# An attention and gated-MLP block on one core: last additions on GpSimd, one weight scale a run later, the first rows in another order

## The chip, the cores and the metric

The kernel runs on one core of a Trainium2 chip, alone. The metric is the device time in microseconds (us); a time shown is the median of several runs. Besides these there is one profiled execution with a trace of every engine: TensorE (PE, with its weight loads PEld), VectorE (DVE), ScalarE (ACT), GpSimd (POOL) and SyncE (SP, which here only starts transfers). "Span" is the time from the first to the last instruction of that execution.

## The reference

Every output row is the input row plus an attention result, gated by an MLP:

```python
x  = A_x                                   # 1 x 2048 x 640
xn = layernorm(x)
q  = xn @ wq                               # 32 heads of 192
k, v = last 512 rows of the caches         # per head
o  = softmax(q @ k.T * 192 ** -0.5) @ v
s  = concat(o) @ wo                        # 6144 -> 640
h  = sigmoid(xn @ w_gate) * (xn @ w_up)    # 640 -> 1536
g  = silu(h @ w_down)                      # 1536 -> 640
return x + s * g
```

## The kernel before, in words

The order of the instructions on each engine is the order in which the program writes them; nothing is rearranged by a scheduler. Each engine works through its own list and waits on semaphores where an operand is not there yet. The program has four stages.

**Head and MLP (lines 273 to 541).** The 2048 rows are 16 tiles of 128. `load_x` (299) starts a transfer for each of the first four tiles on SP, between those of the first slices of the gate and up weights (`load_w`, 320); 324 to 332 set the order: x0, x1, gate 0, up 0, x2, gate 1, up 1, x3, gate 2, and so on. `ln_part` and `ln_stats` (346, 351) compute the statistics of a tile in two halves on DVE, `ln_sqrt` (392) the root on ACT, then follow the reciprocal and `ln_apply` (360) on DVE. `turn` (397) transposes the five 128-column blocks of the normalised tile on PE and copies them from PSUM to SBUF on ACT: for tile 0 in two copies, else in one. `first_mm(q, f)` (383) makes ten 128x128 products of row tile q with feature block f, five for gate and five for up. The loop at 407 weaves these for the first four tiles; `warm_up` (375) puts products of zeros on PE ahead of the first row and behind its transposes (`NWARM`, line 59). From feature block 3 on, all products are 512 columns wide (line 484), with a sigmoid on ACT (489) and a product on DVE (490) behind each.

**Attention (563 to 954).** 16 runs r = 0 to 15: eight groups of two head pairs, each for two halves of the rows (pi 0 and 1). A run has 16 slots k of score products (`stage_s`, 652, exponential on ACT, 667), woven with the query products of the next run (`products`, 569, whose results DVE copies or adds, lines 590 and 607), and then eight blocks of value products (`stage_pv`, 669), each with a division on DVE (683, 684), and a transpose and a store issued on SP (690, `store_o`, 693). `phase_s` (828) hangs other work on slots: in even runs `load_k` (157) on SP at slot 2 and `scale_k` (167) on DVE at slot 12 (14 in one of them), in odd runs the transposes of K (173), loads for later stages and so on.

Weights and keys are scaled by powers of two; for the query weights there is one scale for two groups. `scan_abs` (201) sums absolute values on ACT; `set_scan` (204) and `set_scale` (207) reduce them on DVE, write a 128x128 tile `mx_b` and have SP transpose it into `mx_row` (213); `set_scale2` (215) reduces that row on DVE and writes the scale and its inverse. The tables `sets` and `sets2` (750, 751) say in which (run, slot) the two parts stand. Scale 2 is for groups 4 and 5; its first user is `weights(4, 0)` (755) behind the second value block of run 5, on ACT and then on GpSimd.

**Output products (956 to 1167).** The output and down projections, 24 steps, each of seven block products (`product`, 1003, line 1007) on PE; `result` (1033) finishes one half (LEFT or RIGHT, 320 columns) of a row tile. In steps whose tile is finished it adds a part kept in SBUF (1060), multiplies by scale and gate (`gated`, 990, line 991) and adds `acc` (1062), all on DVE. Usually GpSimd starts the store of a whole tile (1066); in the last step SP starts one for each half (1064). The last half of the last step is made and finished in two quarters of 160 columns (1156 to 1159).

Of the kernel before, what the change touches and what calls it, by code (L numbers as in the profile page):

```python
# [9 lines left out]
ALU = mybir.AluOpType  # L10
# [7 lines left out]
def kernel(  # L18
# [13 lines left out]
    nc = tc.nc  # L32
    P = 128
    ctx.enter_context(tc.manual_schedule())

    xf = A_x.flatten_outer_dims()
    of = out.flatten_outer_dims()
    S, D = xf.shape
# [12 lines left out]
    NCD = D // P  # L51
# [4 lines left out]
    G = 2  # L56
    NG = NPAIR // G
    assert NG == 8 and HQDH == 48 * P and NST == 4
    NWARM = (9, 2)
    FA = 3  # L60
    PC = 3
    GC = 2 * G * DH
# [29 lines left out]
    DN = D // 2  # L92
    LEFT, RIGHT = slice(0, DN), slice(DN, D)
# [179 lines left out]
    with ExitStack() as bctx:  # L273
# [24 lines left out]

        def load_x(t):
            x_sb = xin_pool.tile([P, D], BF16, name=f"x_sb{t}")  # L300
            nc.sync.dma_start(x_sb[:], xf[t * P:(t + 1) * P, :])
            x_tiles[t] = x_sb[:]

        def load_x4(s):
# [15 lines left out]
        def load_w(w_sb, w_r, k):  # L320
            f = slice(f_cuts[k], f_cuts[k + 1])
            nc.sync.dma_start(w_sb[:, :, f], w_r[:, :, f])

        load_x(0)
        load_x(1)
        for k in range(len(f_cuts) - 1):
            load_w(wg_sb, wg_r, k)
            load_w(wu_sb, wu_r, k)
            if k < 2:
                load_x(2 + k)  # L330
            elif k == 3:
                load_x4(1)
# [13 lines left out]
        def ln_part(t, i):  # L346
            if i == 0:
                stats_t[t] = bwork.tile([P, nsub, nc.vector.BN_STATS_DIM], F32, name="stats")
            nc.vector.bn_stats(stats_t[t][:, i, :], x_tiles[t][:, i * fsz:(i + 1) * fsz])  # L349

        def ln_stats(t, i0=0):
            for i in range(i0, nsub):
                ln_part(t, i)
            nc.vector.bn_aggr(mv[:, t, :], stats_t[t][:])
# [5 lines left out]
        def ln_apply(t):  # L360
            xn = xpool.tile([P, D], BF16, name="xn")
            cuts = [0, 2 * P, D] if t == 0 else [0, D]
            for d in map(slice, cuts, cuts[1:]):
                nc.vector.tensor_scalar(  # L364
                    xn[:, d], x_tiles[t][:, d], mv[:, t, 0:1], rstd[:, t, :],
                    op0=ALU.subtract, op1=ALU.mult,
                )
            return xn
# [6 lines left out]
        def warm_up(n):  # L375
            for _ in range(n):
                nc.tensor.matmul(w_ps, lhsT=warm[:, 0:P], rhs=warm[:], start=True, stop=True)

        warm_up(NWARM[0])

        gu_first = [bank2() for _ in range(FA)]

        def first_mm(q, f):
            r = slice(q * P, (q + 1) * P)
            for i, w in enumerate((wg_sb, wu_sb)):
                for c in range(NCD):
                    nc.tensor.matmul(  # L387
                        gu_first[f][:, i, r], lhsT=w[:, c, f * P:(f + 1) * P], rhs=xnT[0][:, c, r],
                        start=(c == 0), stop=(c == NCD - 1),
                    )  # L390

        def ln_sqrt(q):
            nc.scalar.activation(
                rstd[:, q:q + 1, :], mv[:, q:q + 1, 1:2], AF.Sqrt, bias=eps_t[:], scale=1.0
            )

        def turn(q):
            pT = pT_banks[:, q % 2, 0:NCD * P // 2].bitcast(BF16).rearrange("p (c n) -> p c n", c=NCD)
            for c in range(NCD):
                nc.tensor.transpose(pT[:, c, :], xn_t[q][:, c * P:(c + 1) * P], ident[:])  # L400
            for cs in ((slice(0, 2), slice(2, NCD)) if q == 0 else (slice(0, NCD),)):
                nc.scalar.activation(xnT[0][:, cs, q * P:(q + 1) * P], pT[:, cs, :], AF.Copy)

        xn_t = {}
# [2 lines left out]
        for q in range(TQ):  # L407
            if q + 1 < TQ:
                ln_part(q + 1, 0)
            nc.vector.reciprocal(rstd[:, q:q + 1, :], rstd[:, q:q + 1, :])  # L410
            xn_t[q] = ln_apply(q)
            if q + 1 < TQ:
                ln_stats(q + 1, 1)
                ln_sqrt(q + 1)
            if q == 0:
                turn(0)
                warm_up(NWARM[1])
                continue
            first_mm(q - 1, 0)
            turn(q)  # L420
            first_mm(q - 1, 1)
            if q == 2:
                first_mm(0, 2)
                first_mm(1, 2)
            elif q == 3:
                first_mm(2, 2)
        for f in range(FA):
            first_mm(TQ - 1, f)
# [43 lines left out]
        for s in range(NST):  # L472
# [4 lines left out]
            for f in range(NF):  # L477
# [16 lines left out]
                if s + 1 < NST:  # L494
                    t = (s + 1) * TQ
# [251 lines left out]
    scans_pv.update({(4 + n, 7): 15 + n for n in range(NCD)})  # L747
    scans_load = {(0, 6): (11, 5), (1, 4): (12, 4), (2, 4): (13, 5), (3, 4): (14, 4)}
    scans_load.update({(4 + n, 4): (15 + n, 5 - n % 2) for n in range(NCD)})
    sets = {(1, 1): 1, (4, 1): 2, (9, 1): 3}  # L750
    sets2 = {(1, 12): 1, (5, 0): 2, (9, 12): 3}
    scale_s = {0: 2, 3: 3, 15: 4}
    q_after = {1: (0,), 2: (1,), 3: (2,), 4: (3,), 5: (4,), 6: (5, 6), 8: (7,), 10: (8,), 12: (9,), 14: (10,)}

# [24 lines left out]
    def tiles_of(j):  # L779
        kind, m = steps[j]  # L780
        if kind == "D":
            return (m, TQ + m) if m < TQ else (TQ + m, 2 * TQ + m)
        pi, q = divmod(m % 8, TQ)
        return [(2 * pi + i) * TQ + q for i in range(2)]
# [175 lines left out]
    acc = {t: acc_pool.tile([P, D], F32, name=f"acc{t}") for t in order}  # L960
# [29 lines left out]
    def gated(dst, src, gate):  # L990
        nc.vector.scalar_tensor_tensor(dst, src, descale, gate, op0=ALU.mult, op1=ALU.mult)  # L991
# [21 lines left out]
    def keep(b, dst):  # L1013
        nc.scalar.activation(dst, ps_all[:, b, 0:DN], AF.Copy)
# [9 lines left out]
    NP = len(steps)  # L1024
    tmp_at = [0, 0, 0]

    def turn_of(k, rows_):
        tmp_at[k] += 1
        return rows_[(tmp_at[k] - 1) % len(rows_)]
# [3 lines left out]
    def result(j, i, d, b, more, n0=0, n1=DN):  # L1033
        kind, m = steps[j]
        t = tiles_of(j)[i]
        ps, tt = ps_all[:, b, n0:n1], nc.vector.tensor_tensor
        if kind == "D":
            if t not in gate_of:
                gate_of[t] = turn_of(1, gate_rows)
            if more is not None:  # L1040
                v = turn_of(2, down_tmps)
                tt(v, ps, more[:], ALU.add)
                ps = v
            nc.scalar.activation(gate_of[t][:, d], ps, AF.Silu, scale=g_scale)
            if (i, d) in ((0, RIGHT), (1, LEFT)):
                nc.gpsimd.dma_start(gB_d[t * P:(t + 1) * P, :], gate_of[t])
            return
        d = slice(d.start + n0, d.start + n1)
        if m < 8:
            if more is None:  # L1050
                keep(b, acc[t][:, d])
            else:
                tt(acc[t][:, d], ps, more[:], ALU.add)
            return
        gate, o_sb = gx_rows[1, t]
        tmp = turn_of(0, tmps)[:, 0:n1 - n0]
        if more is None:
            gated(tmp, ps, gate[:, d])
        else:
            tt(tmp, ps, more[:], ALU.add)  # L1060
            gated(tmp, tmp, gate[:, d])
        tt(o_sb[:, d], tmp, acc[t][:, d], ALU.add)  # L1062
        if j == NP - 1:
            nc.sync.dma_start(of[t * P:(t + 1) * P, d], o_sb[:, d])
        elif (i, d) in ((0, RIGHT), (1, LEFT)):
            nc.gpsimd.dma_start(of[t * P:(t + 1) * P, :], o_sb)

# [30 lines left out]
    for j in range(NP):  # L1098
# [38 lines left out]
        side(j, 3)  # L1137
        product(j, Z, "A12", 3, True)
        result(j, 0, LEFT, Z, p1s)
        scales(4)  # L1140
        side(j, 4)
        product(j, X, "S3", 4, False)
        result(j, 1, RIGHT, X, p5s)
        scales(5)
        if more:
# [6 lines left out]
        side(j, 6)  # L1152
        product(j, Y, "S4", 5, False)
        result(j, 0, RIGHT, Y, u2s)
        side(j, 7)
        cuts = (0, DN) if more else (0, DN // 2, DN)
# [42 lines left out]
```

## Time and profile before

| what | value |
|---|---|
| runs of the kernel before | 871.42 us median of 3 (871.37 to 873.0) |
| profiled execution, its own time | 872.36 us |
| its span | 870.2 us |
| granted TensorE clock, mean | 0.999 |
| busy: PE, PEld, DVE, ACT, POOL | 863.0, 570.7, 674.5, 628.5, 234.3 us |
| first 512-column product of the MLP (L484) | 14.93 us |
| last product on PE begins / last DVE instruction ends | 866.0 / 867.48 us |
| last store issued (SP, L1064) | 867.51 us |

The times in the table's last three rows, and all times in timelines below, count from the start of the span. A line of a timeline reads: start in us, duration in us, engine, line of the program, operation, tile written <- tiles read, shapes, count of merged instructions, and in brackets how long the engine sat idle before and what released it. "SPq" is the time that SP's sequencer spends on starting a transfer. In the chain that ended last, each instant of the span is put down to the one instruction or transfer that the end was waiting for.

### The profile page before, as it was taken

To read this page: it belongs to the slowest core of one execution; us is meant where nothing else is said; L and a number is where in the kernel's file an instruction comes from. 1 tells how busy PE (TensorE), PEld (TensorE's weight loads), DVE (VectorE), ACT (ScalarE), POOL (GpSimd) and SP (SyncE) were. 2 spreads that over 40 slices of the span, in tenths; PEclk is the share of its full clock that TensorE was granted. 3 is DMA by queue.
4 is the path that set the end of the run, shared out by engine and by line. 5 is a ranking of instruction groups with operands and counts; after the bars stand their busy time and mean duration, and the time that the engine had idled before them with its cause. 6 is when DMAs were issued, how large, how long until landed. Compare 5 with 4: busy or idle time off the path is not lost.

```text
span 870.2 us, 19053 instructions
## 1 busy us (share of the span) xinstructions
PE 863.0 (99%) x7557; PEld 570.7 (66%) x7557; DVE 674.5 (78%) x1148; ACT 628.5 (72%) x783; POOL 234.3 (27%) x320
## 2 busy tenths in 40 slices
PE   9999999999999999999999999999999999999998
PEld 5444447576678676676676676676777777777775
DVE  6586767777877867867877867888788778889997
ACT  4766568899799799799789688647556566766552
POOL 0085076062362352352352452300000011000000
PEclk9999999999999999999999999999999999999999
DMA  9894993998998987998988967997795977676641
GB/s 280 188 248 113 240 244 82 236 138 236 219 158 233 256 170 194 223 172 225 206 144 214 199 106 193 237 206 248 163 277 179 300 240 224 212 269 222 226 134 35
DMA packets 258872, 175.97 MB, mean 202 GB/s; under 512 B 162976, under 2 KB 241440, under 8 KB 258784
## 3 DMA queue, kind: packets, MB, share of 16 engines
q1 hardware_dynamic: 253248, 157.26, 73.2%
q0 software_dynamic: 5536, 17.50, 10.0%
q8 instruction: 59, 0.97, 0.5%
q14 instruction: 29, 0.24, 0.1%
HBM read 101.71 MB, written 36.70 MB: 159 GB/s over the span
## 4 chain that ended last, share of the span: by engine, by line
PE 97%; DVE 1%; DMA 1%; SPq 0%; issue 0%; ACT 0%; DVEq 0%
PE ps_all L1007 26%; PE ps_all L569 21%; PE ps_all L677 20%; PE ps_all L663 19%; PE ps_all L484 11%; PE ps_all L387 1%; DMA kraw<-in_A_k_cache_dram 0%; DVE stats L349 0%; DVE arm L991 0%; DMA x_sb<-in_A_x_dram 0%; DVE arm L1062 0%; DVE arm L1060 0%; DVE qp L590 0%; DVE xn L364 0%; SPq L213 0%
## 5 line engine op out<-in xcount | busy, mean ns | idle before, releaser
L667 ACT ACTIVATE E<-ps_all 128x1024 bf16<-128x1024 f32 x256 | 251.4, 1023 | 92.4 <-PE ps_all L663 90.4
L663 PE MATMUL ps_all<-qT,kT 64*128 64x512 bf16 x1536 | 198.1, 376 | 0.0
L677 PEld LDWEIGHTS <-E 128*128 128x128 bf16 x2048 | 169.7, 98 | 9.2 <-issue 9.2
L677 PE MATMUL ps_all<-v_sb,E 128*128 128x193 bf16 x2048 | 174.3, 247 | 0.9 <-DVE qT L607 0.8
L607 DVE TENSOR_TENSOR qT<-ps_all,qp 128x512 bf16<-128x512 f32 x174 | 115.7, 688 | 48.2 <-PE ps_all L569 38.8
L1007 PEld LDWEIGHTS <-mid 128*128 128x128 f16 x1236 | 120.3, 98 | 46.0
L663 PEld LDWEIGHTS <-kT 64*128 64x128 bf16 x1536 | 86.5, 94 | 77.5 <-issue 3.5
L590 DVE COPY qp<-ps_all 128x512 f32<-128x512 f32 x150 | 100.5, 687 | 42.2 <-PE ps_all L569 42.2
L684 DVE TENSOR_TENSOR o_st<-ps_all,rden 128x768 bf16<-128x768 f32 x128 | 122.6, 958 | 4.4
L569 PE MATMUL ps_all<-mid 64*128 64x512 f16 (+1 forms) x840 | 106.3, 376 | 0.0
L569 PE MATMUL ps_all<-mid,arm 64*128 64x512 f16 (+1 forms) x840 | 105.5, 376 | 0.0
L569 PEld LDWEIGHTS <-mid 64*128 64x128 f16 x840 | 50.4, 94 | 42.0 <-issue 1.4
L569 PEld LDWEIGHTS <-arm 64*128 64x128 f16 x840 | 47.1, 94 | 44.6 <-issue 0.2
L1007 PE MATMUL ps_all<-arm,mid 128*128 128x320 f16 x480 | 70.4, 299 | 0.0
L808 ACT ACTIVATE mid<-mid,w_sc 128x1536 f16<-128x1536 bf16 (+1 forms) x43 | 61.4, 1451 | 0.0
L240 ACT ACTIVATE mid<-mid,w_sc 128x1536 f16<-128x1536 bf16 x37 | 58.1, 1571 | 1.1 <-DVE w_sc L218 0.7
L1007 PE MATMUL ps_all<-op,mid 128*128 128x320 f16 (+1 forms) x408 | 58.1, 295 | 0.0
L490 DVE TENSOR_TENSOR hT_sb<-ps_all,sig_sb 128x512 bf16<-128x512 f32 x48 | 32.8, 686 | 28.4 <-PE ps_all L484 20.8
L489 ACT ACTIVATE sig_sb<-ps_all 128x512 bf16<-128x512 f32 x48 | 28.4, 596 | 35.3 <-PE ps_all L484 33.8
L258 POOL TENSOR_TENSOR mid<-mid 128x384 f16<-128x384 f16 x20 | 18.1, 906 | 120.1 <-ACT mid L240 119.1
L1007 PE MATMUL ps_all<-mid 128*128 128x320 f16 x348 | 49.9, 299 | 0.0
L258 POOL TENSOR_TENSOR arm<-mid 128x384 f16<-128x384 f16 x20 | 18.1, 907 | 114.5 <-ACT mid L240 113.5
(183 smaller groups left out, 1093.1 us busy)
## 6 DMA issues: line engine op xcount, KB each, us to landing
oT_d<-oT SPq DMA_DIRECT2D x64, 384.0 KB, 4.9
mid<-oT_d SPq DMA_DIRECT2D x46, 384.0 KB, 4.0
mid<-in_A_wq_dram POOLq DMA_DIRECT2D x64, 192.0 KB, 6.7
arm<-in_A_wo_dram SPq DMA_DIRECT2D x16, 480.0 KB, 6.2
h_d<-hT_sb SPq DMA_DIRECT2D x16, 384.0 KB, 4.4
kraw<-in_A_k_cache_dram SPq DMA_DIRECT2D x32, 192.0 KB, 3.2
v_sb<-in_A_v_cache_dram SPq DMA_DIRECT2D x32, 192.0 KB, 5.5
arm<-in_A_wq_dram SPq DMA_DIRECT2D x15, 384.0 KB, 5.3
```

What stands on the lines that cost most here:

```text
L240: nc.scalar.activation(raw.bitcast(F16), raw, AF.Copy, scale=w_ups[g // 2])
L258: tt(TB, part_w(g, c, a, 1, 1), part_w(g, c, a, 0, 1), ALU.subtract)
L484: nc.tensor.matmul(gu[:, i, :], lhsT=w[:, c, f * P:(f + 1) * P], rhs=xnT[s][:, c, :], start=(c == 0), stop=(c == NCD - 1),)
L569: nc.tensor.matmul(ps_all[:, b, :], lhsT=w(r, c), rhs=x[r, c, :], start=(first and k == 0), stop=(k == len(cs) - 1), skip_group_check=True,)
L590: nc.vector.tensor_copy(dst, part(b))
L607: nc.vector.tensor_tensor(q_out(i, u, pp), part(b), t, ALU.add)
L663: nc.tensor.matmul(ps[:, b, :], lhsT=kT[h, c * PC + j, :], rhs=qT_t[r][i, j][h, pp, :], start=(j == 0), stop=(j == PC - 1),)
L667: nc.scalar.activation(E_t[r, i, pp][:, c, :, :], ps, AF.Exp, scale=scale_qk)
L677: nc.tensor.matmul(o_ps[:, q // 2, q % 2, 0:DH + 1], lhsT=E[:, c, h, q * P:(q + 1) * P], rhs=vt[:, c, 0:DH + 1], start=(c == 0), stop=(c = ...
L684: nc.vector.tensor_tensor(o_st[:, :, h * DH:(h + 1) * DH].rearrange("p (b i) d -> p b i d", b=2), o_ps[:, :, :, 0:DH], rden[:].to_broadcas ...
L808: eng.activation(t, t.bitcast(BF16), AF.Copy, scale=up)
L1007: nc.tensor.matmul(ps_all[:, b, d0:d1], lhsT=a[:, c, :], rhs=w[:, c, d0:d1], start=(start and c == 0), stop=(c == nk - 1), skip_group_chec ...
```

## The change

Four edits, quoted whole:

```diff
-    NWARM = (9, 2)
+    NWARM = (9, 1)
@@ load_x
-            nc.sync.dma_start(x_sb[:], xf[t * P:(t + 1) * P, :])
+            for d in (LEFT, RIGHT) if t == 0 else (slice(0, D),):
+                nc.sync.dma_start(x_sb[:, d], xf[t * P:(t + 1) * P, d])
@@ turn
-            for cs in ((slice(0, 2), slice(2, NCD)) if q == 0 else (slice(0, NCD),)):
+            for cs in (slice(0, 2), slice(2, NCD)):
@@ loop over the first four tiles
             xn_t[q] = ln_apply(q)
+            for f in {1: (0,), 2: (0, 1), 3: (0,)}.get(q, ()):
+                first_mm(q - 1, f)
             if q + 1 < TQ:
                 ln_stats(q + 1, 1)
+            if q == 2:
+                ln_sqrt(3)
+            turn(q)
+            if q < 2:
                 ln_sqrt(q + 1)
             if q == 0:
-                turn(0)
                 warm_up(NWARM[1])
-                continue
-            first_mm(q - 1, 0)
-            turn(q)
-            first_mm(q - 1, 1)
-            if q == 2:
+            elif q == 1:
+                first_mm(0, 1)
+            elif q == 2:
                 first_mm(0, 2)
                 first_mm(1, 2)
-            elif q == 3:
+            else:
+                first_mm(2, 1)
                 first_mm(2, 2)
@@ the tables of the scales
-    sets = {(1, 1): 1, (4, 1): 2, (9, 1): 3}
-    sets2 = {(1, 12): 1, (5, 0): 2, (9, 12): 3}
+    sets = {(1, 1): 1, (5, 1): 2, (9, 1): 3}
+    sets2 = {(1, 12): 1, (5, 12): 2, (9, 12): 3}
@@ result
-        tt(o_sb[:, d], tmp, acc[t][:, d], ALU.add)
+        if j == NP - 1 and more is not None:
+            nc.gpsimd.tensor_tensor(o_sb[:, d], tmp, acc[t][:, d], ALU.add)
+        else:
+            tt(o_sb[:, d], tmp, acc[t][:, d], ALU.add)
         if j == NP - 1:
-            nc.sync.dma_start(of[t * P:(t + 1) * P, d], o_sb[:, d])
+            eng = nc.scalar if i == 0 and d.start > 0 or n0 == 0 and n1 < DN else nc.sync
+            eng.dma_start(of[t * P:(t + 1) * P, d], o_sb[:, d])
```

In words. **Head:** the first tile of x comes in two transfers of 320 columns, so SP starts one transfer more; every tile's transposed rows are copied in two parts; on ACT the copies of tiles 0 and 1 now stand ahead of the root of the next tile, while the root of tile 3 still stands ahead of the copies of tile 2; on PE the product of tile 1 with feature block 1 now stands ahead of the transposes of tile 2, and one product of zeros is left out behind the transposes of tile 0. **Scale 2:** its first part goes from slot 1 of run 4 to slot 1 of run 5, its second part from slot 0 to slot 12 of run 5; on SP the transpose into `mx_row` goes from ahead of run 4's load of K to behind run 5's stores of attention results. **Tail:** in the last step the three additions of `acc` that end whole halves are made by GpSimd; the two additions of the quarters stay on DVE. Of the five last stores, the right half of the first tile and the first quarter of the second are started by ACT, the others by SP as before.

## The prediction

> **What bounds the kernel now.** I read the page first: the chain that ended last, then part 1.
>
> ```profile
> PE 97%; DVE 1%; DMA 1%; SPq 0%; issue 0%; ACT 0%; DVEq 0%
> ```
>
> TensorE sets the time, so an edit can only win where PE waits: some 3% of 870.2 us. The chain in order of time puts these waits in three places, and the change touches all three: the head (before 15.09 us), one place at 271 to 279 us, and the tail after PE's last matmul (861.1 in the chain, 866.0 on the timeline).
>
> Middle. The chain's L663 pieces "1.40" mark where a run starts: run 3 at 221.88, run 4 at 254.60, run 5 at 288.38, run 6 at 321.10. The table by stages (us, PE busy, PEld, DVE, ACT, POOL, clock, DMA share, GB/s):
>
> ```profile
> 221.88:254.60 32.72, 32.72 (x332) 21.99 (x333) 24.67 (x43) 28.44 (x36) 10.53 (x14) 1.00 1.10 217
> 254.60:276.54 21.94, 21.94 (x202) 15.44 (x202) 15.02 (x27) 19.94 (x22) 8.22 (x11) 1.00 1.07 222
> 276.54:288.38 11.84, 10.99 (x132) 10.69 (x132) 10.00 (x18) 9.61 (x12) 8.50 (x12) 1.00 0.68 144
> 288.38:321.10 32.72, 32.72 (x332) 21.92 (x333) 24.56 (x43) 28.43 (x36) 9.61 (x14) 1.00 0.95 209
> ```
>
> Run 4 takes 33.78, its neighbours 32.72. All of the difference lies in its value products (11.84 against 10.77 in the chain of other runs). The timeline there:
>
> ```profile
> 271.92 1.35 SPq L213 DMA_TRANSPOSE mx_row<-mx_b  x1
> 273.33 1.04 SPq L161 DMA_DIRECT2D kraw<-in_A_k_cache_dram  x2
> 276.52 0.93 DVE L170 TENSOR_SCALAR k_sb<-kraw,w_sc 128x768 bf16<-128x768 bf16 x2 [1.19 <-DMA kraw<-in_A_k_cache_dram]
> 278.15 0.69 DVE L607 TENSOR_TENSOR qT<-ps_all,qp 128x512 bf16<-128x512 f32 x1
> 278.89 3.33 PE L677 MATMUL ps_all<-v_sb,E 128*128 128x193 bf16 x38 [0.85 <-DVE qT L607]
> ```
>
> The transpose of scale 2 stands on SP's queue ahead of the load of kraw; scale_k waits for kraw on DVE; the copy and addition that free a PSUM pair stand behind scale_k; PE waits for those.
>
> Head and tail:
>
> ```profile
> 5.96 0.29 ACT L393 ACTIVATE rstd<-mv,eps_t 128x1 f32<-128x1 f32 x1 [1.55 <-DVE mv L354]
> 6.16 0.75 ACT L402 ACTIVATE mid<-ps_all 128x256 bf16<-128x256 bf16 x2
> 8.24 0.49 DVE L349 BATCH_NORM_STATS2 stats<-x_sb 128x6 f32<-128x320 bf16 x1 [0.62 <-DMA x_sb<-in_A_x_dram]
> 9.33 0.28 PEld L400 LDWEIGHTS <-xn 128*128 128x128 bf16 x5 [0.16 <-DVE xn L364]
> ...
> 865.02 0.55 DVE L991 SCALAR_TENSOR_TENSOR arm<-arm,w_sc 128x320 f32<-128x320 f32 x1
> 865.60 0.49 DVE L1062 TENSOR_TENSOR arm<-arm,acc 128x320 bf16<-128x320 f32 x1
> 866.08 0.38 DVE L991 SCALAR_TENSOR_TENSOR arm<-ps_all,w_sc,arm 128x160 f32<-128x160 f32 x1
> 866.50 0.33 DVE L1062 TENSOR_TENSOR arm<-arm,acc 128x160 bf16<-128x160 f32 x1
> 867.15 0.33 DVE L1062 TENSOR_TENSOR arm<-arm,acc 128x160 bf16<-128x160 f32 x1
> ```
>
> The first copy of transposed rows waits behind the second row's root on ACT, though its transposes ran at 5.04; the fourth x tile lands at 8.22 and holds DVE; and in the tail DVE works without a gap from 861.23 to 867.48.
>
> **Middle: the third scale one run later.** Removed from run 4's SP queue: one transpose, 273.33 - 271.92 = 1.41 us. The two kraw issues move to 271.92 and about 272.5. PE needs its 17th value product at 276.54 + 16 x 10.77/128 = 277.89; from the second landing (277.00) to PE (278.89) took 1.89, so a landing by 276.0 removes the stall. With the latency seen here (3.1 us to landing) it lands at 275.6; with run 8's (4.6, behind full queues, no such transpose) at 277.1. I lean on the first: in the window 268 to 278.4, between about 274.2 and 275.8, the DMA engines move only 40 to 195 GB/s, in the slices that hold the transpose, and mostly 280 to 437 around it. Gain 1.0; ends 1.07 and -0.1.
>
> Added to run 5: four small DVE operations in slot 1, three in slot 12, and the transpose on SP (1.1 to 2.2 us, the eight L213 rows) ahead of the scan load, three loads of wo and one of W_down. The next thing on SP is the transpose of K at 306.04, 5.2 us after those issues end, which covers it. Runs 1 and 9 have the same two slots already and last 32.67 and 32.71: cost nothing. The scale's first user is ACT's L240 after the second value block of run 5, some 3 us behind slot 12; without that cover ACT, and GpSimd's sums behind it, would be late.
>
> **Head.** SP gets one more issue ahead of everything: 0.44 us (two x loads took 0.88). x0's halves gain little, since the statistics of both halves must be in before the mean, and DVE's next instruction, the first statistics of x1, stands ahead of x0's reciprocal: x1 landed at 1.21 + 2.6 = 3.8 and now lands 0.3 to 0.44 later, so the first transposes start near 5.3, not 5.04. Then the new order pays: the two copies (0.36 and 0.48) no longer wait for the root, and the first product starts near 5.95, not 6.57. One warm-up matmul less is hidden in that gap. But the third row's transposes still hang on x3: in the trace they began 9.33 - 8.24 = 1.09 after its landing. The queue is full (DMA share 1.0 and more from 4 us on), so x3 is late by what the split loses at the start, 0.3 of 0.44: transposes at 9.62, 0.28 later. By then one more product group (0.56 us, ten matmuls) is done than before: -0.28. The copy of row 2 split in two behind the root gives back 0.13 (its second part ends near 11.25, PE asks at 11.1). Head: -0.15; ends 0 (x3 0.44 late) and -0.43 (not late).
>
> **Tail.** Three additions of 0.49 leave DVE; only the last is on the path, the first two end while PE still works. Without it DVE's next product starts 0.48 earlier; PE's last half is in PSUM by 866.15, early enough. So 0.49 would be won if GpSimd's addition disturbed nothing. It has no row in f32. Nearest: 128x384 f16, two inputs, 0.91. By elements 320 cost 0.76, by bytes 1.51; I take 0.76, the copy-to-addition step (0.50 to 0.91) being one of operands read. (The Trainium skill, GPSIMD Engine Reference, Performance versus the Vector engine, has 4497 ns for 2048 f32 elements, an estimate of 0.70 here, which would change the tail by 0.06.)
>
> It starts 0.09 behind L991 (as L258 behind L240), at 865.66, and ends at 866.42, and there the trace speaks against the change:
>
> ```profile
> 56.55 0.91 POOL L261 TENSOR_TENSOR mid<-mid 128x384 f16<-128x384 f16 x1
> 56.82 1.99 DVE L447 TENSOR_TENSOR mid<-x_odd,mid 64x2560 f16<-64x2560 bf16 x1
> 57.54 2.04 POOL L262 TENSOR_TENSOR mid<-mid 64x384 f16<-64x384 f16 x1
> ```
>
> L447 alone takes 1.47 (its other instance); here it ended at 58.81, as if it had begun at 57.34, 0.12 before GpSimd's end, and L262 then took 2.04 instead of 0.91. Two additions with both inputs in SBUF go one after the other. DVE's addition of the first half is such a one: due at 866.02, it goes at 866.30. From its start to DVE's end took 0.98 (866.50 to 867.48), so 867.28: gain 0.20, not 0.49; at 1.51 a loss of 0.55.
>
> The Trainium skill (SBUF — State Buffer, Who interferes with whom) says the same of a VectorE instruction with two SBUF inputs beside a GpSimd one that reads SBUF: the later one fully waits. By that rule the tail is 0.20, without it 0.49; the rows agree with the rule.
>
> The stores on ACT have no row: 0.33 as on SP, 0.54 as on POOL. At 0.33 the second issue ends at 867.1 and is covered by SP's last at 867.31 (then 1.5 to landing); at 0.54 the tail wins nothing. ACT and POOL are idle there (last busy 860.0 and 859.1).
>
> **Sum.** -1.0 - 0.15 - 0.2 = -1.35: span 870.2 to 868.85; with the 2.16 outside it the profiled run would take 871.0. That run (872.36) is 0.94 above the median of the runs, 871.42, from which I subtract: 870.05. Ends of all terms: -1.99 and +0.65.
>
> **Rivals.** B, all three in full (x3 not late, no blocking): 871.42 - 1.99 = 869.45. For it: GpSimd may be quicker in f32, DMA may catch up; against it: the rows of 57 us.
> C, the middle wins nothing because kraw lands behind the stores wherever it is issued, as in run 8: 871.05. That is the change not doing what it says; the slow slices at 274.2 to 275.8 speak against it.
> E, slower: PE's clock falls back in the head. The first nine warm-up matmuls took 3.87/9 = 0.43 each, five later of that size 1.08, 0.216 each: half speed for the first 3.9 us. With one warm-up less and new gaps (near 0.2 before the first product, 0.6 before the second transposes) PE is idle for more of 5 to 9 us. A half-speed stage as long as the first costs 1.93, two 3.87: 872.0 to 873.9. It decides once the gaps are long enough; 0.47 was not, on this trace.
> By the Trainium skill (TensorE: Matmul & The Clock Gate, Part 1) the clock falls only after an idle window of about 3.4 us; by that rule this rival falls, and no run here has such a gap.
>
> **How the numbers follow.** Forecast 0.50, B 0.27, C 0.14, E 0.09. What a measurement here can tell from no change is about 0.2%, 1.74 us: faster means below 869.68. B gives 0.27 and the low side of the forecast 0.12: 0.39. Slower (above 873.16): the upper part of E, 0.06. Same: 0.55. The range 869.0 to 871.8 takes in B with 0.4 to spare, C and the tail's bad end; about 0.1 is left out on each side. The forecast's own range is 869.5 to 870.7.
>
> **What would show it.** Run 4 at 32.7 to 32.9 and run 5 at 32.7, with no PE wait for L607; if kraw lands after 276 on the old clock, the middle failed. In the head x3's landing near 8.5, third transposes near 9.6, the 512-column products beginning 0 to 0.4 earlier. In the tail GpSimd's last addition at 0.76 and DVE's next addition waiting about 0.3 for it. I am wrong if run 5 grows, if GpSimd's addition takes 1 us or more, or if x3 lands at 8.2.

## The result: 4.8 us slower, and where they lie

| | before | after |
|---|---|---|
| median of the runs beside each other (6 each) | 871.48 us | 876.28 us |
| ratio, 95% interval | | 1.0054, 1.0041 to 1.0067 |
| profiled execution, span | 870.2 us | 874.7 us |
| first 512-column product of the MLP (chain) | 15.09 | 15.59 |
| last product on PE ends | 866.04 | 865.69 |
| last DVE instruction ends | 867.48 | 867.12 |
| last store has landed | 869.0 | 868.65 |
| from there to the span's end | 1.25 us | 6.05 us |

The changed kernel is slower by 0.54%. The table already says where: the work of the end, from PE's last product to the landing of the last store, is done 0.35 us earlier than before, and then the span goes on for 6.05 us instead of 1.25. What counts is that stretch, in which nothing is computed and nothing is moved. In the experiments below a few executions were far longer than the others of their kernel (883.22 and 1134.23 us in `e1_stores_on_sp`, 877.34 in `e12_order_and_scale`, 876.13 in `e2_adds_on_dve`); they are not explained here, and no reading rests on them.

The profile after begins as before. In the page's fourth part, the shares of the chain that ended last:

```profile
PE 96%; DMA 1%; SPq 1%; DVE 0%; ACT 0%; issue 0%; DVEq 0%
```

PE still has nearly all of it, and the chain ends with DVE at 867.12. It does not reach into the last 7.5 us of the span, so no share of this line can tell what they are; the experiments come back to it.

The end of the span in both kernels, as tables by windows (window and its length in us, then busy time and count of PE, PEld, DVE, ACT, POOL, granted clock, DMA share, GB/s). Before:

```profile
867.00:868.00 1.00, 0.00 (x0) 0.00 (x0) 0.45 (x2) 0.00 (x0) 0.00 (x0) 1.00 0.42 115
868.00:869.00 1.00, 0.00 (x0) 0.00 (x0) 0.00 (x0) 0.00 (x0) 0.00 (x0) 0.75 0.17 41
869.00:870.20 1.20, 0.00 (x0) 0.00 (x0) 0.00 (x0) 0.00 (x0) 0.00 (x0) 0.50 0.00 0
```

After:

```profile
867.00:868.00 1.00, 0.00 (x0) 0.00 (x0) 0.12 (x1) 0.00 (x0) 0.00 (x0) 1.00 0.45 125
868.00:869.00 1.00, 0.00 (x0) 0.00 (x0) 0.00 (x0) 0.00 (x0) 0.00 (x0) 1.00 0.16 39
869.00:870.00 1.00, 0.00 (x0) 0.00 (x0) 0.00 (x0) 0.00 (x0) 0.00 (x0) 1.00 0.00 0
...
873.00:874.00 1.00, 0.00 (x0) 0.00 (x0) 0.00 (x0) 0.00 (x0) 0.00 (x0) 0.50 0.00 0
```

In both the last bytes move in the window that ends at 869. Before, one short row follows. After, six follow, all with five idle engines and no DMA; the granted clock falls to 0.5 in the last five, where PE has nothing to do, and some 4.6 us at 0.5 are enough to pull this execution's mean clock to 0.997.

The tail itself, in the timeline after (start, duration, engine, line, operation, and in brackets how long the engine sat idle and what released it):

```profile
863.66 0.86 POOL L1068 TENSOR_TENSOR arm<-arm,acc 128x320 bf16<-128x320 f32 x1 [0.71 <-DVE arm L996]
...
864.66 0.55 DVE L996 SCALAR_TENSOR_TENSOR arm<-arm,w_sc 128x320 f32<-128x320 f32 x1
865.29 0.86 POOL L1068 TENSOR_TENSOR arm<-arm,acc 128x320 bf16<-128x320 f32 x1 [0.76 <-DVE arm L996]
865.73 0.38 DVE L996 SCALAR_TENSOR_TENSOR arm<-ps_all,w_sc,arm 128x160 f32<-128x160 f32 x1 [0.51 <-PE ps_all L1012]
866.15 0.32 DVE L1070 TENSOR_TENSOR arm<-arm,acc 128x160 bf16<-128x160 f32 x1
866.18 0.86 ACTq L1073 DMA_DIRECT2D out_dram<-arm  x2
...
866.80 0.32 DVE L1070 TENSOR_TENSOR arm<-arm,acc 128x160 bf16<-128x160 f32 x1
```

The last two of GpSimd's three additions take 0.86 each. DVE's first-quarter product at 865.73 waits 0.51 for PE's last product (865.69). ACT starts its two stores within 0.86; SP starts the last one at 867.15, in 0.33. No instruction here is late; yet GpSimd's last one ends at 866.15, where before its last one was a store's start that ended at 859.12.

The runs of the attention, same columns as the windows above, to set against the four rows shown with the prediction:

```profile
255.04:276.98 21.94, 21.94 (x202) 11.35 (x203) 15.43 (x25) 20.00 (x22) 8.22 (x11) 1.00 0.99 232
276.98:287.75 10.77, 10.77 (x130) 10.61 (x132) 8.71 (x16) 9.54 (x12) 7.58 (x11) 1.00 0.64 114
287.75:320.46 32.71, 32.71 (x332) 21.91 (x333) 24.96 (x47) 28.43 (x36) 10.53 (x14) 1.00 1.08 212
320.46:353.65 33.19, 32.88 (x332) 21.98 (x333) 24.24 (x40) 29.55 (x33) 16.28 (x22) 1.00 0.92 206
```

Run 4 (the first two rows) takes 32.71 instead of 33.78, with PE busy throughout, and run 5 takes 32.71, where it had 32.72. Run 6 takes 33.19, which it did not before. In the chain after, in order of time, that is

```profile
337.19 0.92 SPq L161
...
338.17 4.09 DMA kraw<-in_A_k_cache_dram
...
342.28 0.42 DVE k_sb L170
342.70 0.61 DVE qp L595
...
343.41 0.70 DVE qT L612
...
344.15 9.49 PE ps_all L682 x112
```

The load of kraw lands at 342.26, so scale_k on DVE, the copy and the addition behind it and PE's value products come late: the same wait as run 4 had before, two runs on.

The head, timeline after:

```profile
2.71 0.49 DVE L350 BATCH_NORM_STATS2 stats<-x_sb 128x6 f32<-128x320 bf16 x1 [1.43 <-DMA x_sb<-in_A_x_dram]
...
3.75 0.49 DVE L350 BATCH_NORM_STATS2 stats<-x_sb 128x6 f32<-128x320 bf16 x1 [0.54 <-DMA x_sb<-in_A_x_dram]
...
6.28 0.77 ACT L403 ACTIVATE mid<-ps_all 128x256 bf16<-128x256 bf16 x2 [1.46 <-PE ps_all L401]
...
6.94 0.49 DVE L350 BATCH_NORM_STATS2 stats<-x_sb 128x6 f32<-128x320 bf16 x1 [0.61 <-DMA x_sb<-in_A_x_dram]
...
8.04 0.45 PE L401 MATMUL ps_all<-ident,xn 128*128 128x128 bf16 x5 [0.34 <-DVE xn L365]
```

The two lines of before to set against the last two:

```profile
5.93 0.49 DVE L349 BATCH_NORM_STATS2 stats<-x_sb 128x6 f32<-128x320 bf16 x1
...
7.40 0.44 PE L400 MATMUL ps_all<-ident,xn 128*128 128x128 bf16 x5
```

The statistics of x0's first half begin at 2.71, those of the second wait for its landing until 3.75; before, the whole tile was in at 2.93. The statistics of x2 wait 0.61 for its landing and begin at 6.94; before, they began at 5.93 and had no wait. The copies leave at 6.28 without waiting for a root, as planned, but the second transposes start at 8.04 instead of 7.40.

### The profile page after: what moved, and what is told of

The parts are those of the page before. It is cut to its first block, busy times and chain, and to the rows that moved or that the text cites. A ratio compares the mean times of both kernels' runs of the same rounds, so it can differ in the third digit from the quotient of the medians.

```text
span 874.7 us, 19044 instructions
## 1 busy us (share of the span) xinstructions
PE 862.9 (99%) x7547; PEld 566.9 (65%) x7556; DVE 672.6 (77%) x1145; ACT 628.6 (72%) x786; POOL 236.9 (27%) x323
## 4 chain that ended last, share of the span: by engine, by line
PE 96%; DMA 1%; SPq 1%; DVE 0%; ACT 0%; issue 0%; DVEq 0%
PE ps_all L1012 26%; PE ps_all L574 21%; PE ps_all L682 20%; PE ps_all L668 19%; PE ps_all L489 11%; PE ps_all L388 1%; DMA kraw<-in_A_k_cache_dram 0%; DMA x_sb<-in_A_x_dram 0%; DMA mid<-xn 0%; ACT E L672 0%; SPq L702 0%; SPq L302 0%; PE ps_all L401 0%; SPq L323 0%; SPq L161 0%
## 5 line engine op out<-in xcount | busy, mean ns | idle before, releaser
L574 PEld LDWEIGHTS <-mid 64*128 64x128 f16 x840 | 48.2, 94 | 44.2 <-issue 1.0
```

Source lines behind the costliest of these rows:

```text
L574: nc.tensor.matmul(ps_all[:, b, :], lhsT=w(r, c), rhs=x[r, c, :], start=(first and k == 0), stop=(k == len(cs) - 1), skip_group_check=True,)
```

## Experiments

### Which half of the tail's edit: the stores or the additions

Both start from the changed kernel. `e1_stores_on_sp` gives ACT's two stores back to SP:

```diff
-            eng = nc.scalar if i == 0 and d.start > 0 or n0 == 0 and n1 < DN else nc.sync
-            eng.dma_start(of[t * P:(t + 1) * P, d], o_sb[:, d])
+            nc.sync.dma_start(of[t * P:(t + 1) * P, d], o_sb[:, d])
```

> The changed kernel with one thing undone: all five last stores are started by SP again, the three additions stay on GpSimd. In the trace of the changed kernel PE, DVE and the last store are each about 0.36 us earlier than before, and the loss lies behind the last landing: 6.05 us to the end of the span where it was 1.2. Theory Q (the two stores on ACT bring a transfer queue into use that must be closed at the end): the 4.85 are gone, 871.4 or a little less, against 871.5 for the kernel before. Theory G (GpSimd's additions as its last work delay the end): no change, 876.2. Half each: about 873.8.

Measured: 876.53 us, ratio to before 1.007 (1.0039 to 1.0101), span 874.7. Nothing came back, so the stores on ACT do not carry the loss. GpSimd's last addition ends at 866.18 there, 8.55 before the span's end (874.73).

`e2_adds_on_dve` keeps the stores on ACT and gives the three additions back to DVE:

```diff
-        if j == NP - 1 and more is not None:
-            nc.gpsimd.tensor_tensor(o_sb[:, d], tmp, acc[t][:, d], ALU.add)
-        else:
-            tt(o_sb[:, d], tmp, acc[t][:, d], ALU.add)
+        tt(o_sb[:, d], tmp, acc[t][:, d], ALU.add)
```

> The changed kernel with one thing undone: the three last additions are on DVE again, the two stores stay on ACT. Theory Q: 876 or a little more, 6 us from the last landing to the end of the span. Theory G: about 871.3. On either, if the first quarter's product on DVE waited for PE's very last product and not for GpSimd, DVE ends 1.4 us behind PE as in both kernels, so the additions on GpSimd win nothing.

Measured: 872.49 us (ratio to before 1.0012, 1.0002 to 1.0023). So 3.8 of the 4.8 us hang on three additions for which only the starts of three stores waited, none of them the last store. The median spans are 4.15 apart (874.5 with the additions on GpSimd, 870.35 without); the difference is given back outside the span, where the changed kernel has 1.8 us and this one 2.15.

The profiled execution of this kernel shows something else, in the head. PE's timeline, then the windows:

```profile
7.16 0.44 PE L388 MATMUL ps_all<-mid,wu_sb 128*128 128x128 bf16 x5
8.36 0.71 PE L401 MATMUL ps_all<-ident,xn 128*128 128x128 bf16 x5 [0.76 <-DVE xn L365]
```

```profile
7.00:8.00 1.00, 0.60 (x8) 0.43 (x7) 0.70 (x3) 0.12 (x1) 0.00 (x0) 1.00 1.19 263
8.00:9.00 1.00, 0.64 (x7) 0.64 (x8) 0.91 (x3) 0.00 (x0) 0.00 (x0) 0.63 1.14 234
9.00:10.00 1.00, 1.00 (x12) 1.00 (x11) 0.49 (x1) 0.89 (x3) 0.00 (x0) 0.50 1.10 262
...
11.00:12.00 1.00, 1.00 (x15) 1.00 (x13) 0.57 (x4) 0.30 (x1) 0.00 (x0) 0.66 1.06 318
12.00:13.00 1.00, 1.00 (x21) 1.00 (x19) 0.40 (x1) 0.63 (x2) 0.00 (x0) 1.00 0.98 312
```

PE has waited 0.76 for the second row's normalisation, and in the window from 8 on the granted clock falls to 0.63, then 0.50, and is back only near 11.7. A group of five 128-column products goes from 0.28 to 0.53 us, from one start to the next, and the first 512-column product begins at 17.13 instead of the 15.59 of the changed kernel, whose head is the same code. It is rival E, and it came in this execution and not in that one. It accounts for 1.5 us of some executions, not for the 4.8 us of all.

### What on GpSimd costs it: reads beside DVE, arithmetic, or any work at all

The three that follow start from the kernel before. `e5_first_add_only` moves only the first of the three additions, which ends while PE still has 2.8 us to work:

```diff
-        tt(o_sb[:, d], tmp, acc[t][:, d], ALU.add)
+        if j == NP - 1 and (i, d) == (0, LEFT):
+            nc.gpsimd.tensor_tensor(o_sb[:, d], tmp, acc[t][:, d], ALU.add)
+        else:
+            tt(o_sb[:, d], tmp, acc[t][:, d], ALU.add)
```

> The kernel before; of the last step's additions only the first one is on GpSimd, it should end 2.7 us before PE's last product does. With two theories left for the 4.85 us behind the last landing. Theory C (a closing time): after its last work GpSimd needs about 8.5 us until the program can end, hidden where that work ends early; in the changed kernel 866.15 to 874.7. Then the span ends 5.8 us behind PE's end instead of 4.16: 1.6 us longer, 873.0. Theory F (a fixed price of any addition on GpSimd in the last step): 4.85 longer, 876.3. Theory L (only an addition whose result is waited for at the very end costs): no change, 871.4.

Measured: 873.04 us, ratio 1.0017 (1.0005 to 1.0028), span 871.5. GpSimd's one new line in the timeline:

```profile
862.11 0.85 POOL L1063 TENSOR_TENSOR arm<-arm,acc 128x320 bf16<-128x320 f32 x1 [3.32 <-issue]
```

It ends at 862.97, and the span ends 8.55 later (871.52). PE ends at 865.71 and the last store as in the kernel before, so an addition that is finished 2.75 before PE is sets the end of the program.

`e6_store_from_gpsimd` does no arithmetic on GpSimd; it starts the third of the last stores there:

```diff
-            nc.sync.dma_start(of[t * P:(t + 1) * P, d], o_sb[:, d])
+            eng = nc.gpsimd if i == 0 and d.start > 0 else nc.sync
+            eng.dma_start(of[t * P:(t + 1) * P, d], o_sb[:, d])
```

> The kernel before; the third last store (right half of the first tile) is started by GpSimd instead of SP, no arithmetic there. It should be issued about 0.9 us behind PE's end. Theory C for any work of GpSimd: the span ends 8.5 us behind that issue, 5.2 longer than before, 876.7. Theory C for arithmetic alone: only the slower landing of such a store (3.7 us) shows, about 1 us longer, 872.5.

Measured: 876.72 us, ratio 1.0059 (1.0037 to 1.0082), span 875.2. In its timeline:

```profile
866.07 0.54 POOL L1065 DMA_DIRECT2D out_dram<-arm  x1 [7.26 <-DVE arm L1062]
```

End 866.61, 8.62 to the span's end (875.22).

`e7_tiny_copy_at_end` adds one copy of a single column behind the last addition; nobody reads what it writes:

```diff
+            if n1 == DN and n0 > 0:
+                seen = small.tile([P, 1], BF16, name="seen")
+                nc.gpsimd.tensor_copy(seen[:], o_sb[:, d.stop - 1:d.stop])
```

> The kernel before, and behind the last addition on DVE a copy of a single column (128x1) on GpSimd whose result nobody uses. Theory C: whatever its size, the span ends about 8.5 us behind this copy, 6 us longer than before, 877.4. If the price is one of the f32 additions with two inputs, no change, 871.4.

Measured: 877.72 us, ratio 1.0069 (1.0046 to 1.0092), span 875.5. In its timeline:

```profile
866.60 0.19 POOL L1067 COPY seen<-arm 128x1 bf16<-128x1 bf16 x1 [8.49 <-DVE arm L1062]
```

0.19 us of work that is off every path costs 6.1 us (877.72 against 871.61 beside it). End 866.78, 8.77 to the span's end (875.55).

Five kernels, three kinds of work, GpSimd's last end between 862.97 and 866.78: from there to the span's end 8.54 to 8.77 every time. Counted from the start of that work the distances spread from 8.9 to 9.4, so it is the end that counts. The three times that theory C gave beforehand, 873.0, 876.7 and 877.4, are met within 0.4.

What fills this time is in the traces. A timeline shows the work of the engines and leaves out instructions that only wait or flush. Asked for the last line of the program, which closes it, the profile has one of these on GpSimd. Before, then after (count, then least, median and most ns, first and last start):

```profile
L1194 POOLq DRAIN  x3: 40/160/8316, 858.6 to 870.0; - x3
L1203 POOLq DRAIN  x3: 40/93/8666, 865.3 to 874.4; - x3
```

The longest DRAIN is the first of the three and the next thing on GpSimd behind its last work. In the trace before it lasts until 866.88, 7.76 after the end of GpSimd's last store start; in the trace after until 873.92, 7.77 after the end of its last addition. In all fourteen traces of this study this distance is 7.75 to 7.99. In the trace after, the other engines have come to the closing line by 869.22; GpSimd's next instruction there starts 0.04 after the DRAIN ends, and the span ends some 0.78 after it, as in all five kernels above. So the span ends at the later of two times: 1.25 to 1.69 after the last landing, or some 8.6 after GpSimd's last work, of which the DRAIN is 7.8. Before, the second was 859.12 + 8.6 = 867.7, hidden 2.5 us below the actual end of 870.2. Why the DRAIN lasts as long after a copy of one column as after three additions, no run here shows.

> The kernel before, unchanged, for a second trace. Its 27 timed executions have spans of 869.0 to 871.1, median 869.3; the one that the prediction was made from has 870.2 and a wait of 1.07 us in run 4. If the typical execution lacks that wait, this one shows run 4 at 32.7 to 32.9 us and a span near 869.3; if the wait belongs to the kernel, run 4 at 33.8 again.

`e8_before_again` is the kernel before, unchanged, once more: span 869.5, which is also the median span of those 27 executions (not 869.3); GpSimd's last work ends 11.1 before it, which the rule allows, since here the last landing sets the end. Its run 4 takes 32.96, not the 33.78 of the first trace. That is the next question.

### The scale's move by itself

`e4_scale_only`, from the kernel before:

```diff
-    sets = {(1, 1): 1, (4, 1): 2, (9, 1): 3}
-    sets2 = {(1, 12): 1, (5, 0): 2, (9, 12): 3}
+    sets = {(1, 1): 1, (5, 1): 2, (9, 1): 3}
+    sets2 = {(1, 12): 1, (5, 12): 2, (9, 12): 3}
```

> The kernel before with only the move of the third scale. In the changed kernel run 4 went from 33.78 to 32.71 us and run 8 from 32.91 to 32.71, but run 6 from 32.71 to 33.19. Theory 1, the move itself makes run 6 late (one transfer less ahead shifts the phase of SP's queue): the same three numbers here, 870.7. Theory 2, run 6 is late by the head's 0.44 us or by chance of the queues: run 6 stays at 32.7 and the kernel takes 870.2 to 870.4.

Measured: 872.03 us, ratio 1.0004 (0.9994 to 1.0013): no gain. Its profiled execution has run 4, 6 and 8 all at 32.71 or 32.72 and a span of 868.9, 1.3 below that of before, of which run 4 gives 1.07 and run 8 0.20; but it was the fastest of ten. The fourteen traces of this study explain it. With the scale in its old place (nine traces) run 4 exceeds 32.71 by 1.07, 0.52, 0.51, 0.34, 0.25, 0.17, 0.10, 0.10 and 0.06: the trace I predicted from had the largest of them, and the middle one is a quarter of it. With the scale in its new place (five traces) run 4 has no excess, but run 6 exceeds by 1.83, 0.48, 0.40, 0 and 0, through a late kraw where it does; with the old place run 6 has an excess in one of nine, of 0.84. So the wait was removed where it stood, it was small in the usual execution, and waits of the same kind stand in other runs of other executions (run 10 of `e3_head_only`, below, takes 34.47 where others have 32.84, behind a kraw that lands at 474.73). Whether the move makes those in run 6 more frequent, five traces don't settle. What sets the wait in run 4 is when SP comes to the second load of kraw. Counted from the start of the run that is 17.4 to 18.2 in the traces that lose 0.06 to 0.17, 18.3 to 18.7 in those that lose 0.25 to 0.52, and 19.3 in the one that lost 1.07; with the scale moved it is 14.5 to 16.8, and nothing is lost.

### The head

`e3_head_only` makes all edits of the head on the kernel before (the first four hunks of the change).

> The kernel before with only the four edits of the head. The first 512-column product began at 14.93 before and 0.44 later in the changed kernel. If the head alone is the cause, PE reaches the attention stage 0.44 us later and the kernel takes 871.9. If the scale's move reached back, less. My forecast for this part was 0.15 us less than before.

Measured: 872.39 us, ratio 1.0009 (0.9999 to 1.0018). The first 512-column product begins at 15.76, where the trace of before had 15.09 and that of `e8_before_again`, the same kernel, 15.36. Two edits are mixed in it; the next two separate them. `e9_split_only`:

```diff
-            nc.sync.dma_start(x_sb[:], xf[t * P:(t + 1) * P, :])
+            for d in (LEFT, RIGHT) if t == 0 else (slice(0, D),):
+                nc.sync.dma_start(x_sb[:, d], xf[t * P:(t + 1) * P, d])
```

> The kernel before with only the first tile of x in two transfers. In the changed kernel the second half landed at 3.75 us (the whole tile at 2.93 before), so the mean and everything behind it came 0.4 later, and the fourth tile 0.55 later. If the split is what costs the head: the 512-column products begin 0.4 to 0.6 us later than 14.93, 872.0. If it is free: 871.5.

`e10_order_only` is `e3_head_only` without this hunk: the new order, the split copies, one product of zeros less.

> The kernel before with the head's new order, the copies in two parts and one warm-up product less, but the first tile in one transfer. If the order is good and only the split bad: fourth tile at 8.2, third transposes at 9.4, 512-column products 0.3 to 0.45 earlier than 14.93, and 871.1. If the clock falls back here too (the fewer products of zeros leave PE idle more of 5 to 8 us), some executions are 1.5 to 2 us longer with a mean clock of 0.998, and the median is near 871.5.

Measured: the split alone 872.71 us, ratio 1.0015 (1.0006 to 1.0023); the order alone 871.14 us, ratio 0.9996 (0.9987 to 1.0004), with the 512-column products from 15.04 in its trace: 0.05 earlier than in the first trace of before, 0.32 earlier than in the second. `e12_order_and_scale` adds the scale's move to `e10_order_only`.

> The two parts that could be good together: the head's new order without the split, and the third scale one run later; the tail as before. If both help: 871.1 less what the typical execution loses in run 4 (0.25 us in the second trace of the kernel before), 870.8. If the scale's move only shifts the wait to another run: 871.1.

Measured: 871.26 us, ratio 1.0 (0.9988 to 1.0013): the scale's move adds nothing here either.

How the split acts is read from the chain in order of time (start, duration, piece). All of the head's edits, `e3_head_only`:

```profile
3.18 3.91 DMA x_sb<-in_A_x_dram
...
7.11 0.49 DVE stats L350
...
7.70 0.46 DVE xn L365
...
15.76 4.26 PE ps_all L489 x19
```

The same head with x0 in one transfer, `e12_order_and_scale`:

```profile
2.71 3.66 DMA x_sb<-in_A_x_dram
...
6.40 0.49 DVE stats L349
...
7.11 0.46 DVE xn L364
...
15.16 4.91 PE ps_all L488 x22
```

One more start on SP (0.47 with the gap behind it) puts the load of x2 at 3.18 instead of 2.71; it takes 3.91 instead of 3.66, DVE waits for it in both, and what is behind it keeps about its distance: 8.65 and 8.76 from the statistics of x2 to the first 512-column product. In the traces that is 0.6 us (15.76 against 15.16; `e10_order_only` has 15.04). In `e9_split_only`, with the old order, the statistics of x2 begin at 6.64 and the products at 15.76, 9.12 apart, and in `e8_before_again` 9.01: beside those the new order is worth some 0.3 to 0.4.

The medians of `e9_split_only` and before differ by 1.2. In the head its one trace has 15.76, where the six traces of the old order with x0 in one transfer have 15.05 to 15.57: 0.2 to 0.7 of it. Another 0.43 lies at the other end of the program; the rest, 0.1 to 0.6, one trace does not settle. SP closes it with a row of waits for the transfers, 0.06 each, in a fixed order. With one transfer more, the last store signals another semaphore, which stands further ahead in that row: in `e9_split_only` SP is past the wait for it at 869.06 with seven waits still to go, in the trace of before it was the last in the row (869.01). So the span ends 1.68 or 1.69 after the last landing in the four traces with the split where the landing sets the end, and 1.25 to 1.27 after it in the five without it. In the changed kernel this 0.43 is hidden under GpSimd's DRAIN.

`e11_head_more_warm` asks whether the clock's fall in the head is part of that loss. It is `e3_head_only` with four products of zeros behind the first transposes instead of one:

```diff
-    NWARM = (9, 1)
+    NWARM = (9, 4)
```

> All four edits of the head, but four products of zeros behind the first transposes where the change has one. In the run with the additions on DVE the granted clock fell to 0.5 from 8.4 to 11.6 us, with PE busy 2.09 of the 3.4 us before; here PE would be busy for some 0.6 more. If too little work there is the cause: no execution with a mean clock of 0.998 (head alone: one of ten, with the additions on DVE: three of ten), median near 872.0 (0.44 of the split stays). If it is chance: as many as before.

Measured: 872.29 us, ratio 1.0009 (1.0 to 1.0017), granted clock 0.999 or 1.0 in all eleven runs, where `e3_head_only` had 0.998 in one of ten and `e2_adds_on_dve` 0.998 or less in three of ten. The medians of `e3_head_only` and this one differ by 0.1: the fall of the clock is not what the head's loss consists of, and with so few falls the cure is not shown either. A mean of 0.998 is also a weak sign: the trace of `e5_first_add_only` has it from the longer end alone, with the clock at 1.0 all through the head.

No version here is faster than the kernel before by more than its interval; the nearest is `e10_order_only`.

## Why the prediction was wrong

**The step that failed** is the tail's: "so 867.28: gain 0.20, not 0.49; at 1.51 a loss of 0.55". It counts to DVE's end, adds the 1.5 us to the last landing, and takes the rest of the span as given, as if it hung on the last store alone. What work on GpSimd in the last 11 us does to the end of the program is a term that it put at nothing. Both bounds were taken from what GpSimd's addition lasts and whom it disturbs. The cost measured is that GpSimd works late at all: 8.6 us from its last work to the end, 7.8 of them its DRAIN, against 1.25 from the last landing. 866.15 + 8.55 = 874.7. None of the rivals was near it, and the mechanism of the slower one was another. The prediction read GpSimd as idle there ("last busy 860.0 and 859.1"); the trace of before had its DRAIN until 866.88, an instruction that a timeline leaves out and the list for line 1194 has.

**Tail, on DVE.** Forecast: DVE gains 0.20. Measured: 0, counted from PE's last product (1.44 to DVE's end before, 1.43 after, 1.44 in `e2_adds_on_dve` with the additions back on DVE). The addition that was taken away ended at 866.09 in the trace of before, and PE's last product at 866.04: two chains that arrive within 0.05 us of each other. I wrote that PE's last half was "in PSUM by 866.15, early enough"; it was the next bound, at once: in the trace after, DVE's product starts 0.04 behind it, as it did before. GpSimd's addition took 0.86, forecast 0.76 (bounds 0.76 and 1.51). The blocking of DVE by GpSimd's reads, which I took from the rows at 57 us, is not decided: DVE's first-quarter addition came due 0.04 before GpSimd's last addition ended, at 866.15. The Trainium skill (SBUF — State Buffer, Who interferes with whom) also states that blocking; no run here shows it at the end of the program. The stores on ACT (0.38 and 0.44 to start, forecast 0.33) were hidden, as forecast.

**Middle.** Forecast -1.0, and run 4 measured -1.07 in the trace, with run 5 unchanged. The mechanism was right: with the transpose out of the way SP comes to kraw earlier (16.8 into the run in `e4_scale_only`, 18.3 in `e8_before_again`). But in the trace after it comes at 14.5, 4.8 earlier than in the trace of before, and the transpose is only 1.4 of that; by these starts this execution would have had no wait without the move either, so that its -1.07 hits the forecast is in part luck. Two things were wrong with the term. It was measured in an execution of 872.36 and subtracted from a median of 871.42, the time of executions in which this wait, by the middle of nine traces, is a quarter as long; and a wait for kraw came back in run 6 (0.48). Rival C, kraw late wherever it is loaded, has part of it: right in its result, at another run than it named.

**Head.** Forecast -0.15, measured +0.5 in the trace, and +0.9 in the median with the head's edits alone, of which 0.43 is the longer row of waits at the program's end, a term that the prediction did not have. In the head itself the failed step is "the third row's transposes still hang on x3". I followed the fourth tile's landing and priced the extra issue there at 0.3. The same issue delays x2, whose statistics had no wait in the trace of before (5.93) and now bind; x3's began at 8.79 (forecast 8.5), but PE was busy without a pause from 9.34 on. The trace that I predicted from hid this: in `e8_before_again` x2's landing binds as well (6.35). The gain of the new order that I counted against it is 0.3 in the median and within its interval of nothing.

**Rival E** I gave little, on a rule of the Trainium skill (TensorE: Matmul & The Clock Gate, Part 1) that the clock falls after an idle window of some 3.4 us; that it falls only then was my reading. The trace of `e2_adds_on_dve` disagrees: it fell with no gap over 0.76 us, after 3.4 us (4.8 to 8.2) in which PE was busy for 2.09. How little work it takes is not settled: in the trace of `e1_stores_on_sp` PE was busy for 2.18 of the same stretch, and the clock stayed at 1.0. My price, 1.93, compares with 1.54 measured. The same page of the Trainium skill goes on, in the section "A second HAM failure mode: psum-queue depth-cycling", to tell of a clock that goes up and down through frequent short idle times, in a kernel of 512-column products that cycles through PSUM banks. The products here have 128 columns, so it comes nearer than the rule without being this case, and I had not weighed it.

In medians the parts add up: +3.8 for GpSimd's additions, +1.2 for the split, -0.3 for the order, nothing clear of its interval for the scale, 4.7 of 4.8. (The prediction's own totals are off by 0.02: 871.42 - 1.35 is 870.07, not 870.05, and B and C come to 869.43 and 871.07. Nothing hangs on it.)

## What to carry to other kernels

Before you hand late work to an engine that has been idle, ask what the program still does after that engine's last instruction: here a single column copied by GpSimd near the end costs 6 us, and by these traces its last work is free only if it ends some 7.4 us before the last store lands (8.6 less 1.25). Idle in a timeline does not mean free: ask the profile for the line that closes the program too. When a profile shows a wait, take a second trace of the same kernel before you price its removal, and subtract it from the time of the execution that has it. When an instruction leaves a path, look for the next arrival within a few hundredths of a microsecond: it, not the duration removed, is the gain.

## What the runs showed of the chip

- In these kernels the span does not end earlier than about 8.6 us after the last work on GpSimd: 8.54 and 8.55 after an addition of 0.86, 8.55 after one that ended 2.75 before PE did, 8.62 after a store's start, 8.77 after a copy of 0.19. A DRAIN on GpSimd takes 7.75 to 7.99 of it, in all fourteen traces, and costs nothing where it ends before the last landing.
- Each wait for transfers that SP makes in closing the program takes 0.06 us; where the last store's comes eighth from the end of that row and not last, the span ends 0.43 us later.
- PE's granted clock can fall to 0.50 for about 3.4 us in a stage with gaps of at most 0.76 us, in one execution and not in another of the same instructions.
- An f32 addition of 128x320 with two SBUF inputs takes GpSimd 0.86 us, DVE 0.49.
